# A planned attention and two-layer kernel: new durations and lags in the planner, and 32 subtractions moved from GpSimd to VectorE

## The chip, the cores and the metric

The kernel runs on one core of one Trainium2 chip. The metric is the device time of one execution in microseconds (us); where several executions were timed, their median. TensorE (PE in the rows), VectorE (DVE), ScalarE (ACT), GpSimd (POOL) and SyncE (SP) each work through a list of instructions of their own, in order, and wait for each other by semaphores. The transfers are issued by SP.

## What is computed

The reference has three parts in a row. `_attn_ref` runs a recurrence over 768 positions for 4 batches and 8 heads of 48 features: the state is multiplied by a complex number of magnitude below one, the product of key and value is added, and the query reads it. `_moe_ref` takes the 3072 rows of 384 features through `x @ w_in` (384 to 2048), a function g of the hidden values, and `g @ w_out` (back to 384). `_moe2_ref` does the same with other weights and another g:

```python
x = attn_out.transpose(0, 2, 1, 3).reshape(B * S, H * D)
h = x @ w_in;  g = np.where(h > 0.0, h, np.exp(np.minimum(h, 0.0)) - 1.0);  x = g @ w_out      # first layer
h = x @ w_in;  g = np.where(h >= 1, h, np.where(h <= -1, 0.0, (h + 1) ** 2 / 4));  y = g @ w_out  # second layer
```

The weights come as 64-bit floating-point numbers.

## The kernel before

The sequence is cut into 6 chunks of 128 positions, and each chunk into two pairs of batches: 12 units of 256 tokens. For a unit, `norm` and `prefix` make the products of the decay along the chunk on VectorE and ScalarE and write the scaled queries and keys (tiles qd, kd, QK). SP then copies these into another layout, Qs and Ks, by twelve transfers per unit (line 432). `attend` does the scores (line 444), the products with the values (454), the transposes of the keys (459) and the new state (463) on TensorE, with the mask multiplied in on VectorE (tile ssb). Its result is split into a high part xhi (a rounded type that TensorE multiplies in one pass) and the rest xlo. `layer1_tasks` takes each unit through the first layer, two hidden tiles of 128 at a time: 18 multiplications of line 201 into bank 0 or 1 (bank_72 and bank_73 in the order's rows), g on ScalarE and VectorE (lines 228 to 234), and 18 of line 211. `layer2_tasks` does the second layer for 6 groups of 512 tokens, one hidden tile at a time (lines 274 to 285).

Every weight tile is also split in two, whi and wlo. `w_tasks` loads the 64-bit words (line 175), shapes 32-bit numbers of them in three steps on VectorE (176, 178, 180), makes whi by a cast on ScalarE (182), and wlo as the difference. For the first layer the difference is made on TensorE (lines 190 and 191) and copied by ScalarE (193). For the second layer, where `lb` is None, GpSimd subtracts (line 184): 16 tiles by 2 halves, 32 instructions. The second layer's weights go into the same tiles whi and wlo as the first layer's, so each can be written only when the last unit of the first layer has used it. The words pass through st, s, r, M, qd and kd, and the 32-bit numbers through wv and ssb.

The order of all this is not written by hand. Each step is added to a `Plan` (class at line 39) with an engine, a duration in ns, a priority and what it reads and writes. `add` turns these into dependences, each with a lag: `SAME` for two steps of one engine, `CROSS` by the engine that waits, `DMA` after a transfer. `place` fills a list schedule with these numbers, forwards and backwards in turn, and `issue` emits the order of the shortest schedule it found. The numbers decide only the order; on the chip the semaphores decide when a step runs. Sixty multiplications by a tile of zeros (line 517) and twelve more (238) have no data to wait for and run where the planner puts them.

Of the kernel before, what the change touches and what calls it, by code (L numbers as in the profile page):

```python
# [16 lines left out]
B, H, S, D = 4, 8, 768, 48  # L17
C = 128
NC_ = S // C
# [14 lines left out]
def ROW(h, e):  # L34
    """Where feature (h, e) of the attention's output lies in the first layer's input."""
    return 32 * h + e if e < 32 else 256 + 32 * (h % 4) + 16 * (h // 4) + (e - 32)


class Plan:
    """A static schedule: tasks are added in an order that is right by itself, with what they read  # L40
    and write. They are placed by a list scheduler with rough durations, forwards and backwards in
    turn, and issued in the order of the shortest schedule found."""

    SAME = {"PE": 0, "DVE": 130, "ACT": 160, "POOL": 130, "SP": 0, "NONE": 0}
    CROSS = {"PE": 330, "DVE": 190, "ACT": 190, "POOL": 200, "SP": 100, "NONE": 0}     # to
    DMA = 1600
# [4 lines left out]
    def add(self, eng, ns, prio, fn, r=(), w=()):  # L51
        after, i = {}, len(self.tasks)             # task: its results are needed
# [61 lines left out]
def dve(n):  # L114
    return 70 + n / 0.96


def actv(n):
    return 95 + n / 1.2
# [3 lines left out]
def attn_moe2_kernel(ctx: ExitStack, tc: tile.TileContext, a, qk, v, w, mask, ident, nat, out):  # L123
# [40 lines left out]
    def w_tasks(add, layer, f, prio, rb, tb, lb=None):  # L164
        # float64 bits -> float32 (24 bits kept) -> a float32r part and the rest
        for p in range(2):
# [16 lines left out]
            if lb is None:  # L183
                add("POOL", 960, prio, lambda hi=hi, lo=lo, t=t: nc.gpsimd.tensor_tensor(
# [7 lines left out]
            add("PE", 800, prio, rest, r=[tk, ("whi", f, p), "ident", "nid"], w=[bkey])  # L192
# [11 lines left out]
    def y_mms(ys, fs, gt, n, lo):  # L204
        # the products with the activations' high part (lo=0) or with their low part
# [9 lines left out]
    def layer1_tasks(add, xhi, xlo, dst, dk, p0, dp, xk):  # L215
        ys = (ya[:, 0], ya[:, 1], yb)
        for p in range(NF // 2):
# [8 lines left out]
            add("PE", 1960, pr, lambda hp=hp, fs=fs: h_mms(hp, fs, xhi, xlo),  # L226
# [9 lines left out]
            if p == 0:  # L236
                # one accumulation group for the two parts of this bank
# [4 lines left out]
            add("PE", 1310, pr - 10, lambda fs=fs, g2=g2: y_mms(ys, fs, g2[0], 256, 0), r=[("ghi", mb)] + WK, w=BK[2:4])  # L242
            add("PE", 650, pr - 10, lambda fs=fs, g2=g2: y_mms(ys, fs, g2[1], 256, 1), r=[("glo", mb)] + WK, w=BK[2:4])
# [8 lines left out]
    def layer2_tasks(add, g, t2, src, sk, dst):  # L252
        # one group of 512 tokens; the first layer's activations come back from DRAM
# [13 lines left out]
        for f in range(NF):  # L267
# [6 lines left out]
            add("PE", 1960, pr + f, lambda hp=hp, f=f: h_mms(o1(hp), (f,), t2("xhi", i), t2("xlo", i)), r=XK + WK[0], w=[BK[hb]])  # L274
# [9 lines left out]
            add("PE", 1310, pr + f - 1, lambda f=f, ghi=ghi: y_mms(ys, (f,), o1(ghi()), 512, 0), r=[("ghi", mb)] + WK[1], w=YK)  # L284
            add("PE", 650, pr + f - 1, lambda f=f, glo=glo: y_mms(ys, (f,), o1(glo()), 512, 1), r=[("glo", mb)] + WK[1], w=YK)
# [7 lines left out]
    # ------------------------------------------------------------ phase 1: attention and the first layer  # L293
    with ExitStack() as c1:
# [7 lines left out]
        # these also hold the second layer's weights as they come  # L302
# [12 lines left out]
        state = T([96, 2, 2, 4, 128], "state")             # (re/im, d), pair of batches, b, pair of heads, e  # L315
# [19 lines left out]
        def norm(u, pr):  # L335
            """a -> the normalised a, in place."""
# [202 lines left out]
        def t2(name, i=0):  # L539
            return 3 if name == "n" else late[name][i]  # L540
# [172 lines left out]
```

## Time and profile before

| What | us |
|---|---|
| median of 3 executions | 1077.87 |
| lowest and highest of the three | 1070.60, 1078.63 |
| span of the profiled execution, first to last instruction | 1070.1 |
| TensorE busy | 1017.8 |
| VectorE busy | 780.3 |
| ScalarE busy | 506.9 |
| GpSimd busy | 41.2 |

The span is the stretch that the profile's rows cover; it lies 0.5 us under the lowest of the timed executions. "Busy" counts the time in which an engine had an instruction at work, and the end of a multiplication is modelled. A row of the timeline gives the start, the duration, the engine, the line, and, in square brackets, how long the engine was idle before it and what ended that wait. The duration of a short VectorE instruction includes a tail that overlaps with the next one, so what a row of such instructions costs is read from the step between their starts.

### The profile page before, as it was taken

The page shows a single profiled execution, that of the slowest core. Times are in us where ns is not written, and L with a number is a line of the kernel's source. Part 1 is how long each engine was busy: PE and PEld are TensorE (multiplying, and loading weights), DVE is VectorE, ACT ScalarE, POOL GpSimd, SP SyncE. Part 2 cuts the span into 40 slices and gives each one's busy share as a digit, 9 for nine tenths or more (in the row PEclk, how much of TensorE's full clock was granted, in tenths as well). Part 3 has the DMA queues.
Part 4 walks back from the last instruction along what each step waited for, and adds up shares of the span by engine and source line. Part 5 has one row for each costly group of instructions (what it writes and reads, how often), then busy time and mean ns, then how long its engine had stood idle before and what let it go on. Part 6 is the DMA issues. An engine that isn't in the chain of part 4 may idle for free.

```text
span 1070.1 us, 18759 instructions
## 1 busy us (share of the span) xinstructions
PE 1017.8 (95%) x7626; PEld 896.3 (84%) x7626; DVE 780.3 (73%) x1501; ACT 506.9 (47%) x942; POOL 41.2 (4%) x37
## 2 busy tenths in 40 slices
PE   4789899999999999999999989899999999999996
PEld 2469799999999999999999987688888888888885
DVE  7979898998999988988835499955454554544443
ACT  5547475565565466555534555433343333433322
POOL 0000000000000000000000044400000000000000
PEclk8699999999999999999999999999999999999999
DMA  8274624634335426346163144001010010000000
GB/s 316 70 165 136 168 57 95 124 75 105 78 98 128 79 91 119 69 99 133 23 145 102 60 151 161 17 1 59 1 59 1 1 59 1 30 0 1 31 1 33
DMA packets 44543, 84.01 MB, mean 79 GB/s; under 512 B 4512, under 2 KB 27808, under 8 KB 44448
## 3 DMA queue, kind: packets, MB, share of 16 engines
q1 hardware_dynamic: 44448, 82.72, 30.3%
q8 instruction: 62, 1.02, 0.4%
q14 instruction: 33, 0.27, 0.1%
HBM read 54.39 MB, written 9.44 MB: 60 GB/s over the span
## 4 chain that ended last, share of the span: by engine, by line
PE 73%; DVE 14%; DMA 5%; issue 3%; ACT 2%; SPq 1%; POOL 0%; DVEq 0%; ACTq 0%
PE bank L201 31%; PE bank L211 31%; PE bank L444 4%; PE bank L454 3%; PE bank L463 2%; DMA Ks<-QK 2%; DMA st<-in_w_dram 2%; DVE wv L178 1%; DVE A L322 1%; DVE wv L180 1%; DMA A<-in_a_dram 1%; PE bank L459 1%; DVE wv L176 1%; DVE mm L322 1%; DVE mo_e L231 1%
## 5 line engine op out<-in xcount | busy, mean ns | idle before, releaser
L201 PE MATMUL bank<-xhi,whi 128*128 128x256 f32 (+1 forms) x864 | 277.6, 321 | 0.7 <-DVE mo_e L231 0.7
L201 PE MATMUL bank<-xlo,whi 128*128 128x256 f32 (+1 forms) x864 | 275.8, 319 | 0.8 <-DVE xlo L322 0.8
L201 PE MATMUL bank<-xhi,wlo 128*128 128x256 f32 (+1 forms) x864 | 275.8, 319 | 0.0
L201 PEld LDWEIGHTS bank<-xhi,whi 128*128 128x128 f32 x864 | 162.9, 189 | 15.3 <-DVE mo_e L231 1.4
L201 PEld LDWEIGHTS bank<-xlo,whi 128*128 128x128 f32 x864 | 162.9, 189 | 14.3 <-DVE xlo L322 1.0
L201 PEld LDWEIGHTS bank<-xhi,wlo 128*128 128x128 f32 x864 | 162.7, 188 | 13.2
L211 PE MATMUL bank<-mo_hi,whi 128*128 128x256 f32 (+1 forms) x768 | 141.4, 313 | 6.5 <-ACT mo_hi L233 3.3
L211 PE MATMUL bank<-mo_lo,whi 128*128 128x256 f32 (+1 forms) x768 | 141.6, 313 | 2.9 <-DVE mo_lo L234 2.8
L211 PE MATMUL bank<-mo_hi,wlo 128*128 128x256 f32 (+1 forms) x768 | 138.9, 309 | 0.0
L211 PEld LDWEIGHTS bank<-mo_hi,whi 128*128 128x128 f32 x768 | 111.4, 188 | 18.6 <-ACT mo_hi L233 4.3
L211 PEld LDWEIGHTS bank<-mo_lo,whi 128*128 128x128 f32 x768 | 110.9, 189 | 14.7 <-DVE mo_lo L234 4.4
L211 PEld LDWEIGHTS bank<-mo_hi,wlo 128*128 128x128 f32 x768 | 110.9, 188 | 8.8
L228 ACT ACTIVATE mo_e<-bank 128x512 f32<-128x512 f32 x96 | 57.4, 597 | 88.8 <-PE bank L201 87.2
L277 ACT ACTIVATE mo_e<-mo_e,b_half 128x512 f32<-128x512 f32 x64 | 46.4, 724 | 87.7 <-DVE mo_e L275 87.5
L231 DVE SCALAR_TENSOR_TENSOR mo_e<-mo_e,bank 128x512 f32<-128x512 f32 x96 | 65.4, 681 | 24.6 <-ACT mo_e L230 24.0
L275 DVE TENSOR_SCALAR mo_e<-bank 128x512 f32<-128x512 f32 x64 | 44.1, 689 | 48.6 <-PE bank L201 48.6
L233 ACT CAST mo_hi<-mo_e 128x512 fp32r<-128x512 f32 x96 | 59.3, 617 | 39.5 <-DVE mo_e L231 34.7
L234 DVE TENSOR_TENSOR mo_lo<-mo_e,mo_hi 128x512 fp32r<-128x512 f32 x96 | 67.4, 702 | 14.4 <-ACT mo_hi L233 11.2
L277 ACT ACTIVATE mo<-mo,b_half 128x512 f32<-128x512 f32 x32 | 23.2, 724 | 88.0 <-DVE mo L275 88.0
L281 DVE TENSOR_TENSOR mo_lo<-mo_e,mo_hi 128x512 fp32r<-128x512 f32 x64 | 44.1, 690 | 27.5 <-ACT mo_hi L280 26.2
L275 DVE TENSOR_SCALAR mo<-bank 128x512 f32<-128x512 f32 x32 | 22.1, 690 | 57.8 <-PE bank L201 57.8
L230 ACT ACTIVATE mo_e<-mo_e 128x512 f32<-128x512 f32 x96 | 60.8, 633 | 1.6
(122 smaller groups left out, 1519.7 us busy)
## 6 DMA issues: line engine op xcount, KB each, us to landing
st<-in_w_dram SPq DMA_DIRECT2D x28, 384.0 KB, 3.8
A<-in_a_dram SPq DMA_DIRECT2D x12, 768.0 KB, 6.0
QK<-in_qk_dram SPq DMA_DIRECT2D x12, 768.0 KB, 4.5
V<-in_v_dram SPq DMA_DIRECT2D x12, 448.0 KB, 5.3
M<-in_w_dram SPq DMA_DIRECT2D x12, 384.0 KB, 4.1
Qs<-qd SPq DMA_DIRECT2D x36, 128.0 KB, 3.9
Ks<-kd SPq DMA_DIRECT2D x36, 128.0 KB, 4.2
Ks<-QK SPq DMA_DIRECT2D x36, 128.0 KB, 4.9
```

The costliest lines, as they stand in the source:

```text
L201: pe.matmul(out=hp[:, j], lhsT=wt[:, ks], rhs=xt[:, k], start=(i == 0), stop=(i == 8))
L211: pe.matmul(out=ys[mt], lhsT=wt[f][:, ms], rhs=gt[:, j], start=(f == 0 and not lo and wt is whi and whole), stop=(f == NF - 1 and lo == 1 ...
L228: add("ACT", actv(512), pr - 200, lambda hb=hb, e=e: act.activation(out=e, in_=hps[hb], func=AF.Relu, scale=-1.0), r=[BK[hb]], w=[("e", mb)])
L230: add("ACT", actv(512), pr - 200, lambda e=e: act.activation(out=e, in_=e, func=AF.Exp, scale=-1.0), w=[("e", mb)])
L231: add("DVE", dve(512), pr - 200, lambda hb=hb, e=e: vec.scalar_tensor_tensor(out=e, in0=e, scalar=-1.0, in1=hps[hb], op0=ALU.add, op1=ALU. ...
L233: add("ACT", actv(512), pr - 200, lambda e=e, ghi=ghi: act.copy(out=ghi, in_=e), r=[("e", mb)], w=[("ghi", mb)])
L234: add("DVE", dve(512), pr - 200, lambda e=e, ghi=ghi, glo=glo: vec.tensor_tensor(out=glo, in0=e, in1=ghi.bitcast(F32), op=ALU.subtract), r ...
L275: add("DVE", dve(512), pr + f - 2, lambda hp=hp, e=e: vec.tensor_scalar(out=e(), in0=hp, scalar1=-1.0, scalar2=1.0, op0=ALU.max, op1=ALU.m ...
L277: add("ACT", actv(512), pr + f - 2, lambda e=e: act.activation(out=e(), in_=e(), func=AF.Square, scale=0.5, bias=b_half), w=[("e", mb)])
L281: add("DVE", dve(512), pr + f - 2, lambda e=e, ghi=ghi, glo=glo: vec.tensor_tensor(out=glo(), in0=e(), in1=ghi().bitcast(F32), op=ALU.subt ...
L444: pe.matmul(out=s_ps[:, j * 128:(j + 1) * 128], lhsT=Ks[:, h, b], rhs=Qs[:, h, b], start=True, stop=True)
L454: pe.matmul(out=o[32 * j:32 * j + 32], lhsT=lhsT, rhs=rhs, start=(not old and not (part and hg)), stop=(old == (c > 0) and not (part and n ...
```

## The change

The planner gets other numbers. The durations of the TensorE steps and of ScalarE are set anew, the lags depend on the engine that waits (`CROSS`) and, where TensorE is the producer, on it too (`FROM`). The lag after a transfer depends on the tile it writes: 4200 ns for Qs and Ks, 3900 for A and V, 2900 for all others, where it was 1600 for every one. The 32 subtractions of the second layer's wlo go from GpSimd to VectorE and are planned with `dve(384)`. No step is added or dropped. Comments are gone, and lines from the class on lie 8 lower at most: line 184 is 192 after the change, 432 is 440, 201 is 209.

```diff
-    SAME = {"PE": 0, "DVE": 130, "ACT": 160, "POOL": 130, "SP": 0, "NONE": 0}
-    CROSS = {"PE": 330, "DVE": 190, "ACT": 190, "POOL": 200, "SP": 100, "NONE": 0}     # to
-    DMA = 1600
+    SAME = {"PE": 0, "DVE": 118, "ACT": 135, "POOL": 130, "SP": 0, "NONE": 0}
+    CROSS = {"PE": 110, "DVE": 128, "ACT": 120, "POOL": 180, "SP": 50, "NONE": 0}
+    FROM = {"PE": 90}
+    DMA = {"Qs": 4200, "Ks": 4200, "A": 3900, "V": 3900}
...
-            lags.append((t, self.DMA if e == "SP" else self.CROSS[eng] if e != eng else self.SAME[e] if data else 0))
-        self.tasks.append((eng, ns, prio, fn, lags))
+            if e == "SP":
+                lag = self.DMA.get(self.tasks[t][5], 2900)
+            elif e != eng:
+                lag = self.CROSS[eng] + self.FROM.get(e, 0)
+            else:
+                lag = self.SAME[e] if data else 0
+            lags.append((t, lag))
+        name = w[0] if w else None
+        self.tasks.append((eng, ns, prio, fn, lags, name[0] if isinstance(name, tuple) else name))
...
-    return 95 + n / 1.2
+    return 70 + n / 1.2
...
-                add("POOL", 960, prio, lambda hi=hi, lo=lo, t=t: nc.gpsimd.tensor_tensor(
+                add("DVE", dve(384), prio, lambda hi=hi, lo=lo, t=t: vec.tensor_tensor(
                     out=lo, in0=t.bitcast(F32), in1=hi.bitcast(F32), op=ALU.subtract), r=[tk, ("whi", f, p)], w=[("wlo", f, p)])
...
-            add("PE", 1960, pr, lambda hp=hp, fs=fs: h_mms(hp, fs, xhi, xlo),
+            add("PE", 2115, pr, lambda hp=hp, fs=fs: h_mms(hp, fs, xhi, xlo),
```

The other TensorE durations change in the same way: 1310 to 1408 and 650 to 706 or 702 for line 211, 800 to 970 for lines 190 and 191, 880 to 910 for the scores, 1190 and 900 to 1010 and 560 for the values, 340 to 300 and 1250 to 1320 for lines 459 and 463.

What this does to the order is shown at three places. The first is SP's list near the program's start, where the queries and keys of the first unit are copied into Qs and Ks (st are weight words on their way in). Before:

```order
L175 DMA st_127<-in_w_dram 128x768
L432 DMA Qs<-qd_144 16x8x256
L175 DMA st_128<-in_w_dram 128x768
L432 DMA Qs<-qd_144 16x8x256 x2
L175 DMA st_127<-in_w_dram 128x768
L432 DMA Ks<-kd_145 16x8x256 x3
L432 DMA Ks<-QK 16x8x256 x3
L432 DMA Qs<-QK 16x8x256 x3
L338 DMA A_151<-in_a_dram 128x1536
```

SP's list at the same place after the change:

```order
L183 DMA st_128<-in_w_dram 128x768
L440 DMA Qs<-qd_144 16x8x256 x3
L440 DMA Qs<-QK 16x8x256 x3
L440 DMA Ks<-kd_145 16x8x256 x3
L440 DMA Ks<-QK 16x8x256 x3
L346 DMA A_151<-in_a_dram 128x1536
```

The second half of Qs moved ahead of both halves of Ks, and the last three transfers are now those of Ks.

The second place is TensorE's list where it first uses them: transposes of keys into bank_79, scores into bank_76, and the zero multiplications into bank_74. Before:

```order
L517 MATMUL bank_74<-zero 128x512 x9
L459 MATMUL bank_79<-id_sb,Ks 128x96 x4
L517 MATMUL bank_74<-zero 128x512 x3
L238 MATMUL bank_74<-zero 128x512
L459 MATMUL bank_79<-id_sb,Ks 128x96 x4
L444 MATMUL bank_76<-Qs,Ks 128x128 x4
L463 MATMUL bank_79<-V_153,kt 96x48 x8
```

TensorE's list there after the change:

```order
L246 MATMUL bank_74<-zero 128x512
L198 MATMUL bank_79<-wv_126,id_sb 128x384
L199 MATMUL bank_79<-whi_100,nid 128x384
L467 MATMUL bank_79<-id_sb,Ks 128x96 x4
L452 MATMUL bank_76<-Qs,Ks 128x128 x4
L467 MATMUL bank_79<-id_sb,Ks 128x96 x4
L452 MATMUL bank_76<-Qs,Ks 128x128 x4
```

The first scores now follow the first four transposes; the zero multiplications and the second four transposes that stood between them moved.

The third place is VectorE's list soon after the last unit's xlo, where the second layer's weights are made beside the last unit's g (mo_e, mo_lo). Before:

```order
L231 SCALAR_TENSOR_TENSOR mo_e_129<-mo_e_129,bank_72 128x512
L176 TENSOR_SCALAR ssb_147<-s_142 128x384
L178 SCALAR_TENSOR_TENSOR ssb_147<-s_142,ssb_147 128x384
L234 TENSOR_TENSOR mo_lo_133<-mo_e_129,mo_hi_131 128x512
L180 SCALAR_TENSOR_TENSOR ssb_147<-s_142,ssb_147 128x384
L231 SCALAR_TENSOR_TENSOR mo_e_130<-mo_e_130,bank_73 128x512
L176 TENSOR_SCALAR ssb_147<-M 128x384
L178 SCALAR_TENSOR_TENSOR ssb_147<-M,ssb_147 128x384
L180 SCALAR_TENSOR_TENSOR ssb_147<-M,ssb_147 128x384
L234 TENSOR_TENSOR mo_lo_134<-mo_e_130,mo_hi_132 128x512
```

VectorE's list there after the change:

```order
L239 SCALAR_TENSOR_TENSOR mo_e_129<-mo_e_129,bank_72 128x512
L186 SCALAR_TENSOR_TENSOR ssb_147<-s_142,ssb_147 128x384
L188 SCALAR_TENSOR_TENSOR ssb_147<-s_142,ssb_147 128x384
L242 TENSOR_TENSOR mo_lo_133<-mo_e_129,mo_hi_131 128x512
L192 TENSOR_TENSOR wlo_112<-ssb_147,whi_96 128x384
L184 TENSOR_SCALAR ssb_147<-M 128x384
L239 SCALAR_TENSOR_TENSOR mo_e_130<-mo_e_130,bank_73 128x512
L186 SCALAR_TENSOR_TENSOR ssb_147<-M,ssb_147 128x384
L192 TENSOR_TENSOR wlo_109<-wv_126,whi_93 128x384
L184 TENSOR_SCALAR wv_126<-s_141 128x384
L242 TENSOR_TENSOR mo_lo_134<-mo_e_130,mo_hi_132 128x512
```

The subtractions (L192) stand between the other steps, each a step or more behind the L188 that finishes its input; GpSimd's list has none left.

## Rows read from the trace of the kernel before

**Rows 1.** The page: span, and TensorE's busy time.

```profile
span 1070.1 us, 18759 instructions
PE 1017.8 (95%) x7626; PEld 896.3 (84%) x7626; DVE 780.3 (73%) x1501; ACT 506.9 (47%) x942; POOL 41.2 (4%) x37
```

**Rows 2.** Six stretches: length, busy us of PE, PEld, DVE, ACT, POOL, clock, DMA.

```profile
0.00:64.63 64.63, 41.16 (x106) 24.54 (x106) 57.02 (x140) 30.82 (x61) 2.01 (x5) 0.79 0.61 181
64.63:80.10 15.47, 14.26 (x153) 12.19 (x153) 10.77 (x31) 9.12 (x21) 0.00 (x0) 0.89 0.59 192
80.10:137.30 57.20, 53.32 (x412) 46.64 (x413) 52.87 (x117) 35.83 (x76) 0.00 (x0) 0.97 0.54 143
137.30:612.85 475.55, 470.15 (x4976) 457.37 (x4975) 399.29 (x816) 260.52 (x510) 1.03 (x1) 1.00 0.42 93
612.85:695.30 82.45, 72.60 (x421) 61.50 (x420) 78.60 (x128) 40.26 (x73) 38.14 (x31) 1.00 0.35 115
695.30:1070.10 374.80, 366.26 (x1565) 294.08 (x1563) 181.73 (x273) 130.32 (x203) 0.00 (x0) 0.99 0.06 20
```

**Rows 3.** SP's timeline, the issues of the first unit's last copies.

```profile
56.94 1.83 SPq L432 DMA_DIRECT2D Ks<-QK  x3
58.87 3.07 SPq L432 DMA_DIRECT2D Qs<-QK  x3
```

**Rows 4.** TensorE's timeline, first use of Ks and Qs.

```profile
64.63 0.68 PE L459 MATMUL bank<-id_sb,Ks 96*128 96x96 f32 x4 [3.60 <-DMA Ks<-QK]
...
66.86 0.85 PE L459 MATMUL bank<-id_sb,Ks 96*128 96x96 f32 x4
67.50 1.46 PE L444 MATMUL bank<-Qs,Ks 96*128 96x128 f32 x8
```

**Rows 5.** VectorE's timeline: first mask multiplication, second xlo of units 0 and 1.

```profile
68.99 0.69 DVE L322 TENSOR_TENSOR ssb<-bank,mask_sb 128x512 f32<-128x512 f32 x1 [5.23 <-PE bank L444]
79.49 0.55 DVE L322 TENSOR_TENSOR xlo<-bank,xhi 128x384 fp32r<-128x384 f32 x1
136.88 0.55 DVE L322 TENSOR_TENSOR xlo<-bank,xhi 128x384 fp32r<-128x384 f32 x1
```

**Rows 6.** What TensorE waited for, 60 to 612 us: total, times, longest.

```profile
PE bank L459 <- DMA Ks<-QK: 3.6, 1, 3.6
PE bank L444 <- DMA Ks<-QK: 2.2, 2, 1.2
PE bank L444 <- DMA st<-in_w_dram: 1.9, 1, 1.9
...
PE bank L444 <- DMA V<-in_v_dram: 0.5, 1, 0.5
```

**Rows 7.** What VectorE waited for, 80.1 to 137.3 us.

```profile
DVE wv L176 <- DMA st<-in_w_dram: 2.6, 3, 1.0
```

**Rows 8.** VectorE's timeline between the layers: long and short instructions of equal form.

```profile
616.20 1.25 DVE L180 SCALAR_TENSOR_TENSOR ssb<-M,ssb 128x384 uint32<-128x384 uint32 x1
...
620.48 0.35 DVE L176 TENSOR_SCALAR wv<-st 128x384 uint32<-128x384 uint32 x1
...
621.82 0.55 DVE L178 SCALAR_TENSOR_TENSOR wv<-st,wv 128x384 uint32<-128x384 uint32 x1
622.28 1.16 DVE L176 TENSOR_SCALAR ssb<-r 128x384 uint32<-128x384 uint32 x1
...
689.63 0.77 DVE L180 SCALAR_TENSOR_TENSOR ssb<-r,ssb 128x384 uint32<-128x384 uint32 x1
```

**Rows 9.** GpSimd's timeline, one of the 32 subtractions.

```profile
621.98 1.25 POOL L184 TENSOR_TENSOR wlo<-wv,whi 128x384 fp32r<-128x384 f32 x1 [2.23 <-ACT whi L182]
```

**Rows 10.** What TensorE waited for, 612 to 700 us.

```profile
PE bank L211 <- ACT mo_hi L233: 3.3, 4, 1.4
PE bank L211 <- ACT mo_hi L280: 3.2, 1, 3.2
```

**Rows 11.** GpSimd's waits over the whole span; the longest is the first.

```profile
POOL wlo L184 <- ACT whi L182: 650.6, 27, 607.3
```

More of the change, by code (lines that the diff above doesn't have):

```diff
@@ L191, in rest @@
                 pe.matmul(out=bk[:, 0:DM], lhsT=nid, rhs=hi, start=False, stop=True)
-            add("PE", 800, prio, rest, r=[tk, ("whi", f, p), "ident", "nid"], w=[bkey])
+            add("PE", 970, prio, rest, r=[tk, ("whi", f, p), "ident", "nid"], w=[bkey])
             add("ACT", actv(384), prio, lambda lo=lo, bk=bk: act.copy(out=lo, in_=bk[:, 0:DM]), r=[bkey], w=[("wlo", f, p)])
@@ L241, in layer1_tasks @@
             WK = [(n, f, 1) for n in ("whi", "wlo") for f in fs]
[L242 to L243 removed]
+            add("PE", 1408, pr - 10, lambda fs=fs, g2=g2: y_mms(ys, fs, g2[0], 256, 0), r=[("ghi", mb)] + WK, w=BK[2:4])
+            add("PE", 706, pr - 10, lambda fs=fs, g2=g2: y_mms(ys, fs, g2[1], 256, 1), r=[("glo", mb)] + WK, w=BK[2:4])
         i = count["st"] % 2
@@ L273, in layer2_tasks @@
             WK = [[(n, f, p) for n in ("whi", "wlo")] for p in range(2)]
-            add("PE", 1960, pr + f, lambda hp=hp, f=f: h_mms(o1(hp), (f,), t2("xhi", i), t2("xlo", i)), r=XK + WK[0], w=[BK[hb]])
+            add("PE", 2110, pr + f, lambda hp=hp, f=f: h_mms(o1(hp), (f,), t2("xhi", i), t2("xlo", i)), r=XK + WK[0], w=[BK[hb]])
             add("DVE", dve(512), pr + f - 2, lambda hp=hp, e=e: vec.tensor_scalar(
@@ L283, in layer2_tasks @@
             YK = [BK[y] for y in yi]
-            add("PE", 1310, pr + f - 1, lambda f=f, ghi=ghi: y_mms(ys, (f,), o1(ghi()), 512, 0), r=[("ghi", mb)] + WK[1], w=YK)
-            add("PE", 650, pr + f - 1, lambda f=f, glo=glo: y_mms(ys, (f,), o1(glo()), 512, 1), r=[("glo", mb)] + WK[1], w=YK)
+            add("PE", 1408, pr + f - 1, lambda f=f, ghi=ghi: y_mms(ys, (f,), o1(ghi()), 512, 0), r=[("ghi", mb)] + WK[1], w=YK)
+            add("PE", 702, pr + f - 1, lambda f=f, glo=glo: y_mms(ys, (f,), o1(glo()), 512, 1), r=[("glo", mb)] + WK[1], w=YK)
         for m in range(3):
@@ L470, in attend @@
                     sb = ssb[sb_i]
-                    add("PE", 880, pr - 50, lambda b=b, hg=hg: scores(b, hg), r=QSB + KSB, w=[BK[4]])
+                    add("PE", 910, pr - 50, lambda b=b, hg=hg: scores(b, hg), r=QSB + KSB, w=[BK[4]])
                     tt(pr - 150, 512, sb, s_ps.rearrange("p (j t) -> p j t", j=4),
                        mask_sb.rearrange("p (o t) -> p o t", o=1).to_broadcast([128, 4, 128]), ALU.mult, [BK[4]], [("ssb", sb_i)])
-                    add("PE", 1190 if c > 0 else 900, pr - 50, lambda b=b, hg=hg, sb=sb: values(b, hg, sb),
+                    add("PE", 1010 if c > 0 else 560, pr - 50, lambda b=b, hg=hg, sb=sb: values(b, hg, sb),
                         r=[("ssb", sb_i), vb] + (QSB + [("state", bp, b)] if c > 0 else []), w=[BK[5 + b]])
```

4 lines of the change are left out of this document (2 added, 2 removed).

## The prediction

> **What bounds the kernel now.** The page comes first: TensorE is busy for 1017.8 of 1070.1 us [rows 1], so all that a new order can win lies in 52.3 us, and the next question is where they lie. I cut the span at the first use of Ks, at the first two finished units, at the end of the first layer's even part and where the second layer begins [rows 2]. Up to 64.63 us TensorE mostly waits for work or multiplies zeros, and VectorE, busy for 57.02, sets the pace together with the copies into Ks and Qs. From 64.63 to 80.10 the first unit goes through the attention in a chain. In the two stretches from 80.10 to 612.85 TensorE loses 57.20 - 53.32 = 3.88 and 475.55 - 470.15 = 5.40. Between the layers, 612.85 to 695.30, it loses 82.45 - 72.60 = 9.85, and there VectorE is the fullest engine: 78.60 of 82.45. From 695.30 on TensorE is busy but for 8.54, most of which is the last transfers and the last checks; VectorE has half its time to spare, and neither the lags after a transfer nor the subtractions matter there. The granted clock is 0.97 to 1.00 of full speed (2.4 GHz) from 80.10 on, so I carry nothing for the clock behind that point; before it, it is 0.79 and 0.89. What ends TensorE's waits I read next [rows 4, 6, 10], then VectorE's timeline around them [rows 5, 7, 8].
>
> **Start.** TensorE's first transposes of Ks begin at 64.63 after 3.60 of waiting for Ks; the first scores follow only at 67.50 [rows 4]. Three zero multiplications, one of line 238 and four more transposes stand between them, and the last Qs are issued after the last Ks, from 58.87 with 3.07 us for the three [rows 3]. In the new order Qs goes ahead of Ks, and the scores come right behind four transposes. The four before them cost the step from 66.86 to 67.50, 0.64. If Ks lands as before, the scores begin at 64.63 + 0.64 = 65.27, 2.2 earlier, and the mask multiplication that waited 5.23 for them [rows 5] with them. From there to the second xlo VectorE has about the same work in both orders, 0.4 less in the new one by the steps of its instructions. Together -2.6. When Ks lands is not known: its three issues took 1.83 and the three of Qs 3.07 [rows 3], so with Qs in front Ks could come some 3 us later (term +0.4), or, if the cheaper place behind Qs costs it nothing and k' is ready sooner, some 2.4 earlier (-5). I take -2.6, since VectorE finishes k' at about the same place in its list.
>
> **First layer.** TensorE's waits that a transfer ends are, behind the first scores, 2.2 + 1.9 + 0.5 = 4.6 [rows 6]. The planner allowed 1600 ns from the end of an issue to the data; the gap from the last Ks issue (56.94 + 1.83 = 58.77) to the transposes at 64.63 is 5.9, so 4200 is nearer to the chip, and it now keeps other work for such times. But from 80.10 to 137.30 VectorE is nearly as full (52.87) as TensorE (53.32), and the next unit's first layer begins with its second xlo, at 136.88 [rows 5]. The new order puts 128 instructions where 117 stood before that one: 11 x 52.87 / 117 = 5.0 us more. It gives TensorE 28 multiplications more ahead of the same place: 28 x 53.32 / 412 = 3.6. So this stretch gains nothing, though three VectorE waits of 2.6 for st [rows 7] shrink. I take -3.5 from the later units alone: 1.9 + 0.5 of transfer waits, some 0.3 of the waits for Ks, and 0.8 of the steps that wait for VectorE because its lag was too long or short in the plan. If the plan's better lags fill every gap that is not VectorE's, it is -9.3 (3.88 + 5.40), and if the 5.0 us fall on the path whole while TensorE's 3.6 cover only part, and nothing else comes, +3: a range of -9.3 to +3.
>
> **Between the layers.** 32 subtractions leave GpSimd; one takes 1.25 there [rows 9]. On VectorE the same shapes step by 0.46 to 0.55 (from 621.82 to 622.28 it is 0.46) [rows 8], so 32 x 0.47 = 15.0 us go onto an engine with 82.45 - 78.60 = 3.85 to spare. Against this stands what GpSimd costs VectorE now: 27 of its instructions last about 0.81 longer than their like, each while a GpSimd subtraction runs, as the step of line 176 at 622.28 (1.16 against 0.35 at 620.48) and those of line 180 at 616.20 (1.25) and, shorter, at 689.63 (0.77) [rows 8]. Summed over the 27 this is 18.1 us. Only instructions that read no bank are hit, those that read one never. The net is 15.0 - 18.1 = -3.1 on VectorE, which is the engine that sets this stretch. In the trace TensorE waits there 3.3 for mo_hi of line 233 and 3.2 for the second layer's first mo_hi [rows 10]; both follow VectorE through mo_e and the weights. With the engine 3.1 lighter, and planned with a duration that is right (960 stood for GpSimd's 1.25), I take both waits as nearly gone: -6.5. All of the 9.85 could go (lower end); if the wait moves to the cast on ScalarE that each subtraction now sits behind, only -2 is left, which I take as the likely upper end; the case beyond it is the second rival. GpSimd waited 650.6 for these casts in all, 607.3 of it before the first [rows 11].
>
> The Trainium skill speaks against this edit on the page "Perfetto Trace Analysis", section "Optimizing Scalar/DVE Operations": where DVE is saturated, work may better go off it, even to GpSimd, though the two share a read port, so that moving work between them might not help. By its first half the edit is +15.0 on the fullest engine; by its second half what GpSimd does is not free for DVE. The lengthened rows show the second half at work here, and 18.1 against 15.0 decides narrowly for the move. [...]
>
> **Second layer.** Its order on TensorE is that of before but for where it begins, and no wait there hangs on a lag that moved: 0, within 1 either way.
>
> **The sum.** -2.6 - 3.5 - 6.5 + 0 = -12.6. The profiled execution spans 1070.1, and so would come to 1057.5. That span lies 0.5 under the lowest of the three runs and 7.8 (0.7%) under their median of 1077.87; the difference applied to the median gives 1065.3, and I forecast 1065.
>
> **Rivals.** First, VectorE bounds the first layer too. For it: 52.87 against 53.32 in the second unit's stretch, and the 11 instructions more. Against it: from 137.30 on it is busy for 399.29 of 475.55 only. Then the start's gain and the stage's are eaten there, and the 6.5 are cut to about 5: 1073.
>
> Second, slower: VectorE works in order, so a subtraction whose cast is late stops what is queued behind it, the steps of mo_e and mo_lo that TensorE waits for. In the new list it often stands only one or two instructions behind the step that finishes its input, while ScalarE needs the cast (and its own queue) in between. GpSimd's waits but the longest come to (650.6 - 607.3) / 26 = 1.67 each, and nobody stood behind it. VectorE can take 3.85 of idle and the 3.1 gained; with the 6.1 of the other terms 13.05 in all, or 0.41 a subtraction. Beyond 0.41 the kernel gets slower. At 0.8, half of what GpSimd had, it is 32 x 0.8 - 13.05 = +12.6: 1090. Against it: the planner knows the cast, with a lag of 120 to 128, and mostly puts another instruction of some 0.5 between.
>
> Third, the numbers change the order and not the time: TensorE's list is bound by the same last wait at each place, and what one transfer no longer costs another does; the four terms then cancel to within 3: 1078, for which the few and short waits of TensorE speak.
>
> **Chances.** The forecast's case 0.68, the first rival 0.18, the second 0.06, the third 0.08. A measurement of this kernel can tell about 1% (10.8 us) from no change. The forecast's case reaches from 1053 (all four terms at their lower ends: -5 - 9.3 - 9.85 - 1 = -25.2) to 1072, and 0.10 of its 0.68 lies above 1067; the first and third rival lie within 1%, but for 0.01 above; the second is slower. So faster 0.58, within 1% 0.35, slower 0.07. The range from 1053 to 1077 leaves out the second rival, half of the third and the forecast's lowest tail.
>
> **What would show it.** Right: the first scores near 65.3 and the second xlo near 76.9; TensorE's waits for Ks, st and V gone but for the first; no VectorE instruction of the lines of 176 to 180 above 0.8 us; GpSimd idle from the start on; TensorE's loss between the layers under 4; the second layer as long as before. Wrong: VectorE's waits for whi at the moved subtraction adding up to more than 6 (second rival); the stretch from the first to the second unit longer than 57.20 by several us (first rival); the first scores later than 67.5, because Ks now lands last; waits for mo_hi of line 233 as long as before.

## The result and the profile after the change

The changed kernel takes 1062.95 us (median of four executions, 1059.36 to 1065.68); the kernel before, with one more execution beside it, 1075.32 (1070.60 to 1078.63). The ratio is 0.9895, with a 95% interval of 0.9856 to 0.9934: faster by 1.05%, or some 12 us. A second job with six executions gave 0.9889 (0.9866 to 0.9912). The forecast was 1065 with a range of 1053 to 1077, that is -12.6 us, and the time lies in it. The sum came out right; of its three terms one was right in kind, and the other two were not. The profiled execution shows how.

The page of the changed kernel, to be read beside [rows 1]:

```profile
span 1063.9 us, 18684 instructions
PE 1020.5 (96%) x7626; PEld 901.5 (85%) x7626; DVE 779.4 (73%) x1533; ACT 507.6 (48%) x942; POOL 2.0 (0%) x5
```

The same six stretches as in [rows 2], cut at the same events (the first use of Ks, the first layer's start in two units, the end of its even part, the second layer's start), though not at the same number of multiplications, as the counts show: length, then busy us of PE, PEld, DVE, ACT, POOL, the granted clock, and the DMA engines' share and rate. The seventh row is a piece of the fourth, right behind a wait.

```profile
0.00:63.66 63.66, 41.38 (x110) 24.61 (x110) 56.54 (x141) 30.03 (x60) 2.01 (x5) 0.79 0.65 185
63.66:80.85 17.19, 16.81 (x145) 14.77 (x146) 10.95 (x35) 8.81 (x21) 0.00 (x0) 0.60 0.43 155
80.85:142.16 61.31, 57.91 (x457) 50.19 (x456) 59.88 (x129) 40.23 (x82) 0.00 (x0) 1.00 0.51 137
142.16:614.59 472.43, 463.11 (x4883) 450.47 (x4882) 392.68 (x793) 254.39 (x496) 0.00 (x0) 0.99 0.44 94
614.59:690.00 75.41, 75.41 (x477) 67.71 (x476) 72.23 (x151) 42.95 (x77) 0.00 (x0) 1.00 0.40 126
690.00:1063.90 373.90, 365.85 (x1564) 293.76 (x1562) 187.11 (x288) 131.17 (x208) 0.00 (x0) 0.99 0.06 20
...
362.08:366.00 3.92, 3.92 (x20) 3.92 (x21) 1.85 (x4) 1.77 (x4) 0.00 (x0) 0.56 0.58 216
```

Read the difference of the first two numbers of a row, which is TensorE's idle time, against [rows 2]: 22.28 for 23.47 at the start, 0.38 for 1.21 in the first unit, 3.40 for 3.88 in the second, 9.32 for 5.40 in the other units, nothing for 9.85 between the layers, 8.05 for 8.54 at the end. Together idle time fell by 8.9 us. But TensorE was busy for 2.7 us more (1020.5 against 1017.8) with the same 7626 multiplications: the clock of the second row is 0.60, where [rows 2] had 0.89, and its busy time is 2.6 us longer. So the span fell by 6.2 only. This profiled execution is the slowest of the four (1065.68), and that of before the fastest (1070.60), so the profile shows half of what the medians show.

Between the layers VectorE now runs like this (its timeline, with the moved subtraction in the second row):

```profile
629.64 0.55 DVE L186 SCALAR_TENSOR_TENSOR wv<-st,wv 128x384 uint32<-128x384 uint32 x1
630.11 0.55 DVE L192 TENSOR_TENSOR wlo<-wv,whi 128x384 fp32r<-128x384 f32 x1
630.58 0.55 DVE L188 SCALAR_TENSOR_TENSOR wv<-st,wv 128x384 uint32<-128x384 uint32 x1
```

The subtraction steps by 0.47 us, as estimated, and no instruction is lengthened as those of [rows 8] were. What VectorE waits for between 605 and 700 us, in all, times, longest:

```profile
DVE wlo L192 <- ACT whi L190: 2.2, 2, 1.2
```

Two of the 32 subtractions wait for their cast, 2.2 us together: the second rival's mechanism is there, at a sixth of the 13 us from which it would have decided.

And in the other units, TensorE's waits from 142 to 615 us, which answer to [rows 6]:

```profile
PE bank L452 <- DMA Ks<-QK: 6.2, 3, 2.3
PE bank L452 <- DVE ssb L330: 1.0, 1, 1.0
PE bank L219 <- ACT mo_hi L241: 0.9, 2, 0.6
```

The waits for st and V are gone. The planner now allows 4200 ns for Ks, and yet the waits for Ks grew from 2.2 to 6.2 us.

### The profile page after: what moved, and what is told of

The parts are those of the page before. It is cut to its first block, busy times and chain, and to the rows that moved or that the text cites. A ratio compares the mean times of both kernels' runs of the same rounds, so it can differ in the third digit from the quotient of the medians.

```text
span 1063.9 us, 18684 instructions
## 1 busy us (share of the span) xinstructions
PE 1020.5 (96%) x7626; PEld 901.5 (85%) x7626; DVE 779.4 (73%) x1533; ACT 507.6 (48%) x942; POOL 2.0 (0%) x5
## 3 DMA queue, kind: packets, MB, share of 16 engines
q8 instruction: 62, 1.02, 0.4%
## 5 line engine op out<-in xcount | busy, mean ns | idle before, releaser
L219 PEld LDWEIGHTS bank<-mo_hi,whi 128*128 128x128 f32 x768 | 111.8, 189 | 11.7 <-ACT mo_hi L241 1.3
L241 ACT CAST mo_hi<-mo_e 128x512 fp32r<-128x512 f32 x96 | 59.4, 618 | 43.7 <-DVE mo_e L239 42.3
L242 DVE TENSOR_TENSOR mo_lo<-mo_e,mo_hi 128x512 fp32r<-128x512 f32 x96 | 65.7, 685 | 11.8 <-ACT mo_hi L241 11.5
L452 PE MATMUL bank<-Qs,Ks 96*128 96x128 f32 x384 | 56.1, 292 | 8.2 <-DMA Ks<-QK 6.2
L288 ACT CAST mo_hi<-mo_e 128x512 fp32r<-128x512 f32 x64 | 39.8, 622 | 46.0 <-DVE mo_e L287 45.8
L452 PEld LDWEIGHTS bank<-Qs,Ks 96*128 96x128 f32 x384 | 50.2, 203 | 11.7 <-issue 6.4
```

Of the source, the lines that this page charges most:

```text
L219: pe.matmul(out=ys[mt], lhsT=wt[f][:, ms], rhs=gt[:, j], start=(f == 0 and not lo and wt is whi and whole), stop=(f == NF - 1 and lo == 1 ...
L241: add("ACT", actv(512), pr - 200, lambda e=e, ghi=ghi: act.copy(out=ghi, in_=e), r=[("e", mb)], w=[("ghi", mb)])
L242: add("DVE", dve(512), pr - 200, lambda e=e, ghi=ghi, glo=glo: vec.tensor_tensor(out=glo, in0=e, in1=ghi.bitcast(F32), op=ALU.subtract), r ...
L288: add("ACT", actv(512), pr + f - 2, lambda e=e, ghi=ghi: act.copy(out=ghi(), in_=e()), r=[("e", mb)], w=[("ghi", mb)])
L452: pe.matmul(out=s_ps[:, j * 128:(j + 1) * 128], lhsT=Ks[:, h, b], rhs=Qs[:, h, b], start=True, stop=True)
```

## Experiments: which half of the change made the gain

**The move alone, and the numbers alone.** The two parts of the diff were run apart. The first kernel is the one before with the new lines for the subtraction only:

```diff
-                add("POOL", 960, prio, lambda hi=hi, lo=lo, t=t: nc.gpsimd.tensor_tensor(
+                add("DVE", dve(384), prio, lambda hi=hi, lo=lo, t=t: vec.tensor_tensor(
```

> Numbers of the kernel before, but the 32 subtractions planned and issued on VectorE. Theory 1, the gain between the layers comes from the move (VectorE freed of the 18.1 us of lengthened instructions, subtraction planned with a true duration): TensorE's waits from the last unit to the second layer's start, 9.9 us before, fall under 4, the time falls by 5 to 10 us, 1065 to 1070. Theory 2, it comes from the new numbers: the waits stay near 10 and the time is that of before within 4 us, 1071 to 1079.

Measured: 1060.59 us, ratio 0.9893 (0.9864 to 0.9922). Its first unit, and its stretch from the last unit into the second layer:

```profile
64.70:83.00 18.30, 18.17 (x152) 16.05 (x152) 9.94 (x28) 8.62 (x20) 0.00 (x0) 0.65 0.46 153
608.50:688.00 79.50, 79.50 (x493) 71.07 (x492) 71.40 (x146) 42.07 (x76) 0.00 (x0) 1.00 0.39 120
```

In the second row TensorE is busy for 79.50 of 79.50: all idle time between the layers is gone, by the move alone, and the time is that of the full change, 11.7 us under the kernel before in the same job, where at most 10 were expected.

Idle time understates this. In the traces of these two kernels TensorE's multiplications have the same order up to number 5535, and again for the last 1442; between these lie the same 649 in two orders. Their stretch in the kernel before, then in the move alone (the rows count two more that reach into it):

```profile
600.04:723.91 123.87, 114.02 (x651) 97.29 (x650) 99.79 (x162) 56.84 (x103) 39.16 (x32) 1.00 0.24 78
602.10:712.50 110.40, 110.40 (x651) 97.15 (x650) 97.47 (x196) 57.61 (x104) 0.00 (x0) 1.00 0.28 86
```

The move made them 13.5 us shorter: 9.85 of that was idle time, and 3.6 stood in TensorE's busy time, though the work and the clock are the same.

The second kernel is the changed one with that edit taken back, so it has the new numbers and GpSimd:

> New numbers, the subtractions left on GpSimd and planned there with 960. Theory 1 (the move makes the gain): about 9 us of TensorE waits between the layers, some 20 VectorE instructions there lengthened by about 0.8 us, and a time of 1070 to 1077, since the rest of the order gave nothing in the changed kernel. Theory 2 (the numbers make it): waits there under 3 us, 1060 to 1066.

Measured: 1085.06 us, ratio 1.0116 (1.0078 to 1.0154). The numbers by themselves make the kernel slower, beyond what either theory expected. TensorE's multiplications have the same order as in the changed kernel, so the stretch between the layers can be cut at the same ones; the changed kernel's stands second. Then follow four instructions of VectorE and two of GpSimd in it:

```profile
613.70:710.07 96.37, 81.71 (x477) 70.23 (x476) 83.96 (x135) 44.68 (x82) 37.63 (x32) 0.96 0.31 99
614.59:690.09 75.50, 75.50 (x478) 67.75 (x476) 72.32 (x151) 43.04 (x77) 0.00 (x0) 1.00 0.40 126
```

```profile
640.53 1.16 DVE L184 TENSOR_SCALAR wv<-s 128x384 uint32<-128x384 uint32 x1
...
643.51 0.35 DVE L184 TENSOR_SCALAR wv<-st 128x384 uint32<-128x384 uint32 x1
...
650.33 0.35 DVE L184 TENSOR_SCALAR wv<-M 128x384 uint32<-128x384 uint32 x1
650.60 0.35 DVE L184 TENSOR_SCALAR wv<-kd 128x384 uint32<-128x384 uint32 x1
```

```profile
640.16 1.31 POOL L192 TENSOR_TENSOR wlo<-wv,whi 128x384 fp32r<-128x384 f32 x1 [1.51 <-ACT whi L190]
641.44 1.13 POOL L192 TENSOR_TENSOR wlo<-ssb,whi 128x384 fp32r<-128x384 f32 x1
```

TensorE is idle for 96.37 - 81.71 = 14.7 us there, 4.8 more than in the kernel before, and the stretch takes 96.37 - 75.50 = 20.9 us longer than in the changed kernel. The two profiled spans, 1084.3 and 1063.9, differ by 20.4: all that this kernel is behind lies between the layers. The instruction at 640.53 lasts 1.16 us while GpSimd subtracts from 640.16 to 641.47; the one at 643.51, of the same form and with GpSimd idle until 643.61, lasts 0.35, as do the last two, which step by 0.27. In this trace 27 VectorE instructions are lengthened, by 18.8 us in all.

**The same order, with either engine.** TensorE's order is shared by those two kernels; VectorE's and ScalarE's differ between the layers, because the planner places a subtraction of 960 ns on GpSimd in another way. To hold everything else still, the changed kernel's plan was kept, and only the call put on GpSimd:

```diff
-                add("DVE", dve(384), prio, lambda hi=hi, lo=lo, t=t: vec.tensor_tensor(
+                add("DVE", dve(384), prio, lambda hi=hi, lo=lo, t=t: nc.gpsimd.tensor_tensor(
```

> The order of the changed kernel word for word, only that GpSimd runs the subtractions at the places planned for VectorE. Theory 1: VectorE loses 32 x 0.47 = 15 us of work and gets back about 18 us of lengthened instructions, of the lines that shape the weights' words above all; net some +3 us on an engine with 3.2 us to spare in 75.4, and GpSimd's 1.25 comes later than 0.47: 2 to 8 us of TensorE waits return, 1065 to 1071. Theory 2 (the order alone matters): no waits, 1061 to 1065.

Measured: 1071.05 us, ratio 0.9971 (0.9946 to 0.9995). The same stretch, cut at the same multiplications:

```profile
614.34:694.81 80.47, 78.05 (x477) 67.86 (x476) 70.67 (x123) 42.23 (x77) 32.22 (x27) 1.00 0.37 118
```

TensorE is idle for 2.4 us where the changed kernel was never idle, and the stretch takes 5.0 us longer (80.47 for 75.50). Twenty instructions are lengthened, by 12.4 us, of which VectorE, 15 us of subtractions lighter, can carry most. The profiled spans, 1069.3 and 1063.9, differ by 5.4, and both first units ran at half clock; so nearly all of the difference is GpSimd's, between the layers. By the medians this kernel is 8 us behind the changed one; where the other 3 us lie was not traced. Of the 20.9 us that the kernel with the numbers alone loses, then, 5.0 come with GpSimd in a given order, and 15.9 with the other order of VectorE and ScalarE that the planner made for it.

The other way round, the order of the kernel before with the call on VectorE, at the places planned for GpSimd:

```diff
-                add("POOL", 960, prio, lambda hi=hi, lo=lo, t=t: nc.gpsimd.tensor_tensor(
+                add("POOL", 960, prio, lambda hi=hi, lo=lo, t=t: vec.tensor_tensor(
```

> The order of the kernel before word for word, planned for GpSimd with 960, only that VectorE runs the 32 subtractions at the places in the program where GpSimd's were issued. If the gain is VectorE's relief from 18 us of lengthened instructions, TensorE's waits between the layers fall to under 5 and the time to 1062 to 1068 although nothing was planned for it. If the plan of the subtraction makes the gain, VectorE waits for ScalarE's casts in front of the subtractions (over 5 us in all) and the time stays at 1070 to 1078.

Measured: 1069.33 us, ratio 0.9939 (0.9915 to 0.9962). The first unit and the stretch between the layers:

```profile
64.70:87.30 22.60, 22.60 (x152) 19.68 (x153) 11.06 (x31) 9.55 (x21) 0.00 (x0) 0.50 0.40 128
612.60:692.20 79.60, 75.92 (x462) 66.76 (x461) 75.45 (x161) 41.97 (x77) 0.00 (x0) 0.98 0.37 120
```

TensorE's idle time between the layers falls from 9.85 to 79.60 - 75.92 = 3.7 with nothing planned for it, and no instruction is lengthened. The time is between the two cases expected. The 649 multiplications from above, which stand here in the order of the kernel before, give the share:

```profile
606.20:725.02 118.82, 114.23 (x651) 98.50 (x650) 96.53 (x194) 57.02 (x103) 0.00 (x0) 0.99 0.25 82
```

They take 118.82 us, 5.1 less than before, where the move alone took 13.5 less; a fall of the clock from 678.6 to 682.0 us is in it, which costs 1.7, so that it would be 6.8 without it. By the ratios it is 0.61% of 1.07%. So about half of the gain is VectorE's relief, and the rest comes with planning the subtraction as VectorE's.

**A truer duration for GpSimd.** Could the planner have been told instead? The kernel with the numbers alone, with 1250 in place of 960:

> New numbers, subtractions on GpSimd, planned with 1250 ns instead of 960, near what they last there. If the 1085 us of the new numbers alone come from the short duration, TensorE's waits between the layers fall from 15 to under 8 and the time to 1070 to 1077. If they come from GpSimd lengthening VectorE's instructions, which no duration of GpSimd tells the planner, about 26 instructions are still lengthened by 0.7 us each, the waits stay at 10 or more and the time at 1078 or more.

Measured: 1084.39 us, ratio 1.0076 (1.0050 to 1.0102).

```profile
615.50:702.30 86.80, 71.73 (x438) 62.55 (x437) 79.33 (x129) 41.92 (x78) 40.57 (x32) 0.94 0.34 109
```

The loss is 15.1 us, 26 instructions are lengthened by 17.5 us, VectorE is busy for 79.33 of 86.80. The second of the expected cases holds: neither 960 nor 1250 ns on GpSimd tells the planner what the subtraction costs, since the cost falls on VectorE's instructions.

## Experiments: the first unit and the clock

In the changed kernel TensorE begins the first unit a microsecond earlier than before, and the scores come 3.5 us earlier than the 67.50 of [rows 4]. Its timeline:

```profile
63.66 0.52 PE L467 MATMUL bank<-id_sb,Ks 96*128 96x96 f32 x4 [1.65 <-issue]
64.02 1.08 PE L452 MATMUL bank<-Qs,Ks 96*128 96x128 f32 x8
64.94 0.56 PE L467 MATMUL bank<-id_sb,Ks 96*128 96x96 f32 x4
65.88 2.08 PE L452 MATMUL bank<-Qs,Ks 96*128 96x128 f32 x8 [0.38 <-DVE ssb L330]
```

The first scores take 1.08 us, the second, of the same form, 2.08: the clock has fallen to half (1.2 GHz), and it stays there until about 79, although TensorE has hardly a gap (16.81 busy of 17.19). This is VectorE's row of the second xlo of the first unit, which [rows 5] has at 79.49:

```profile
80.03 0.56 DVE L330 TENSOR_TENSOR xlo<-bank,xhi 128x384 fp32r<-128x384 f32 x1 [0.30 <-ACT xhi L337]
```

That is 0.5 us later, where the forecast had it 2.6 earlier. In the kernel before, zero multiplications stood behind the first transposes [rows 4], and the clock came back after them, from 0.50 between 66 and 68 us to 1.00 from 70 on. They do not decide it: the move alone and the run with VectorE in GpSimd's place have the order of the kernel before on TensorE here, the same zeros with it, and ran this unit at 0.65 and 0.50 (their rows above). To test whether TensorE's own work decides, eight more of them were put into the wait (the order is otherwise that of the changed kernel):

```diff
             def turn(b, hg):
+                for _ in range(0 if first else 8):
+                    pe.matmul(out=banks[3], lhsT=zero, rhs=zero[:, 0:1].to_broadcast([128, 512]), start=True, stop=True)
+                first.append(1)
```

> The changed kernel with 8 more multiplications of zeros right ahead of the first transposes of Ks, where TensorE stood idle from 62.0 to 63.66 us. If the clock of 1.2 GHz from 65 to 79 us in the changed kernel comes from what TensorE did before, the granted clock of 64 to 79 us rises from 0.6 to 0.85 or more, scores take 1.1 instead of 2.05 us, the first layer starts at 76 to 78 instead of 80.65, and the time falls by 2 to 4 us. Rival: VectorE sets the second unit anyway; then the clock rises but the second unit's first layer still begins near 142 and the time stays within 1 us. Second rival: the clock is not in TensorE's hand here, and nothing changes.

Measured: 1060.08 us, ratio 0.9893 (0.9870 to 0.9916), so no gain that can be told from the changed kernel's. In its profiled execution the first unit ran at full clock, in 11.28 us:

```profile
63.48:74.76 11.28, 10.78 (x144) 9.38 (x145) 10.11 (x33) 8.50 (x21) 0.00 (x0) 1.00 0.66 237
```

But the mean clock of its four executions was 0.986, 0.976, 0.979 and 0.982, and the time followed it (1058.87, 1063.21, 1060.37, 1059.79): one good profile is no proof. The changed kernel itself, run again, settles what the good profile is worth:

> The changed kernel once more, beside the other two on one chip. With the first unit's clock left to chance its executions spread over 4 us or more, 1059 to 1066, at a ratio of 0.987 to 0.992 to the kernel before; the two with zeros spread less. If the spread does not come from there, all three spread alike.

Measured: 1061.57 us (1055.91 to 1065.40), ratio 0.9889. The profiled execution is the fastest of the six. TensorE's timeline of the same four rows, and the first unit:

```profile
63.90 0.52 PE L467 MATMUL bank<-id_sb,Ks 96*128 96x96 f32 x4 [1.19 <-ACT wlo L201]
64.26 1.08 PE L452 MATMUL bank<-Qs,Ks 96*128 96x128 f32 x8
65.18 0.49 PE L467 MATMUL bank<-id_sb,Ks 96*128 96x96 f32 x4
66.12 1.16 PE L452 MATMUL bank<-Qs,Ks 96*128 96x128 f32 x8 [0.45 <-DVE ssb L330]
```

```profile
63.90:75.20 11.30, 10.83 (x145) 9.43 (x145) 9.95 (x32) 8.49 (x21) 0.00 (x0) 1.00 0.66 237
```

The same instructions in the same order, behind a wait of 1.19 us instead of 1.65, and the clock holds: the unit takes 11.30 us where the other execution of the same kernel needed 16.99 (63.66 to its first multiplication of the first layer at 80.65), 5.7 us more. The whole spans are 1054.1 and 1063.9. So this kernel's executions differ by chance in the clock of the first unit: 5.7 of the 9.8 us between these two lie there. The other execution also had a second fall of the clock, from 464.6 to 468.0 us. The next two stretches of the faster one, that is the second unit and the other units:

```profile
75.16:135.70 60.54, 57.81 (x459) 50.54 (x458) 60.35 (x131) 40.05 (x82) 0.00 (x0) 1.00 0.50 139
135.70:604.73 469.03, 461.02 (x4883) 448.77 (x4882) 392.34 (x793) 254.60 (x496) 0.00 (x0) 1.00 0.44 94
```

The kernel before meets the same chance: the 15.47 us of [rows 2] are from the fastest of its executions, while TensorE in the same order took 18.30 and 22.60 us in the two rows named above (19.4 and 22.8 when cut at the same multiplication), and 23 executions of it in one job went from 1070.85 to 1079.53 us.

More zero multiplications, sixteen in a wait of 4.1 us, were then put into the kernel of the move alone:

> Numbers of the kernel before, subtractions on VectorE, and 16 multiplications of zeros ahead of the first transposes of Ks, where TensorE stood idle for 4.1 us. If the clock after that idle time is what made the first unit long (83.0 instead of 79.0 us in the run of the move alone, whose order there is that of before), the granted clock of the first unit is 0.9 or more, its first layer starts at 75 to 78, and the time is 1053 to 1058, under the changed kernel's 1063. Rival: the zeros only fill the wait and the clock falls as before in most runs: 1059 to 1063, as the move alone.

Measured: 1057.20 us, ratio 0.9830 (0.9801 to 0.9858), and its six executions lie within 1.4 us (1056.15 to 1057.57), where the move alone had 5.5 (1058.33 to 1063.82). Its first unit:

```profile
64.60:78.30 13.70, 12.57 (x152) 10.90 (x152) 9.73 (x28) 8.51 (x20) 0.00 (x0) 1.00 0.60 204
```

In these six executions nothing is left of the spread; they are too few to say that the clock cannot fall there.

## Experiments: the waits for Ks

The seventh row of the changed kernel's stretches shows what a wait for Ks costs beside itself. TensorE waited for 2.32 us until 362.08; in the 3.92 us behind it the clock was 0.56, which is 3.92 x 0.44 = 1.7 us more. (Behind the two other long waits for Ks, of 1.97 us at 410.37 and 1.95 at 510.61, the clock stayed whole.) The planned 4200 ns count from the end of an issue, for which the planner has 650, so in the plan a copy lands 4.85 us after its issue begins. The copies from QK take longer as a rule; the medians from issue to landing are the last column of the changed kernel's DMA issues:

```profile
Qs<-QK SPq DMA_DIRECT2D x36, 128.0 KB, 5.1
Ks<-kd SPq DMA_DIRECT2D x36, 128.0 KB, 4.6
Ks<-QK SPq DMA_DIRECT2D x36, 128.0 KB, 5.3
```

So the lag of both was raised in the changed kernel:

```diff
-    DMA = {"Qs": 4200, "Ks": 4200, "A": 3900, "V": 3900}
+    DMA = {"Qs": 6500, "Ks": 6500, "A": 3900, "V": 3900}
```

> The changed kernel with 6500 instead of 4200 ns planned for the copies into Qs and Ks (measured medians from issue to landing 3.8 to 5.3 us, and TensorE waited 6.2 us for Ks in three units). If these waits come from a lag that is still too short, they fall under 2 us, the falls of the clock behind them go too, and the time falls by 5 to 9 us, 1054 to 1058. Rival: the planner's order is of one piece and another number moves the loss elsewhere: other TensorE waits of 4 us or more in the first layer, 1060 to 1066.

Measured: 1063.06 us, ratio 0.9875 (0.9834 to 0.9916). TensorE's waits:

```profile
PE bank L467 <- ACT kt L488: 3.4, 2, 2.2
PE bank L462 <- DVE ssb L330: 3.0, 1, 3.0
PE bank L452 <- DVE ssb L330: 2.0, 3, 0.8
```

No wait for Ks is left, and waits for kt and ssb took their place, as the rival had it; the first unit of its profiled execution ran at 0.65. With ten zero multiplications as above added to it:

> The changed kernel with 6500 ns for Qs and Ks (TensorE's waits in the first layer 12.3 instead of 17.4 us, but a first unit at half clock) and 10 multiplications of zeros ahead of the first transposes. If the clock of the start took what the lag gave, the first unit runs at 0.9 or more, its first layer starts near 76 instead of 87.8, and the time is 1052 to 1057. Rival: the dip that the long lag cost comes from elsewhere and the time stays at 1059 or more.

Measured: 1056.94 us (1055.53 to 1062.17), ratio 0.9846 (0.9822 to 0.9870). The first unit was at 0.81, better than 0.65 and short of the expected 0.9, and one of five executions fell back to 1062. Last, the kernel of the move and sixteen zeros was given the lags of the change, and nothing else of its numbers:

```diff
-    DMA = 1600
+    DMA = {"Qs": 4200, "Ks": 4200, "A": 3900, "V": 3900}
...
-            lags.append((t, self.DMA if e == "SP" else self.CROSS[eng] if e != eng else self.SAME[e] if data else 0))
+            lags.append((t, self.DMA.get(self.tasks[t][5], 2900) if e == "SP" else self.CROSS[eng] if e != eng else self.SAME[e] if data else 0))
```

> The numbers of the kernel before with only the transfer lags of the change (4200, 3900, 2900), the subtractions on VectorE and 16 multiplications of zeros: tells what the lags are worth in a plan that is otherwise that of the fastest run, 1057.2. If lags near the measured landing help by themselves, TensorE's waits that a transfer ends (4.0 in that run) fall under 2 and the time to 1053 to 1056. Rival, as in the changed kernel: the planner trades them for other waits or a low clock, 1056 to 1064.

Measured: 1055.22 us (1054.99 to 1056.37), ratio 0.9819 (0.9802 to 0.9836): the lowest median of all, and faster than the changed kernel (0.9889 in the same job). Against the same kernel without the lags (1057.20, ratio 0.9830, in another job) it is 2 us lower, but the intervals of the two ratios overlap, so that a gain from the lags is not shown. Its stretches from the first unit to the second layer:

```profile
67.60:81.60 14.00, 12.84 (x151) 10.53 (x150) 12.66 (x33) 9.72 (x24) 0.00 (x0) 1.00 0.44 152
81.60:138.40 56.80, 51.77 (x409) 44.55 (x407) 53.74 (x120) 36.22 (x73) 0.00 (x0) 1.00 0.56 140
138.40:604.90 466.50, 463.56 (x4927) 451.06 (x4926) 393.31 (x798) 256.90 (x501) 0.00 (x0) 1.00 0.43 95
604.90:684.30 79.40, 79.40 (x492) 71.00 (x491) 71.97 (x147) 42.80 (x77) 0.00 (x0) 1.00 0.37 120
```

TensorE loses 2.9 us in the third row, where the changed kernel lost 9.3 and the kernel before 5.4, and the clock is full throughout. Its waits behind the start that a transfer ends are 2.3 us, where they were 4.0 without the lags, which is near to the 2 us expected; the wait for mo_lo fell too, from 3.5 to 2.5. Since the planner made another order of the whole from these numbers, the difference can't be put down to one wait.

## Why the prediction was right, point by point

**Start, forecast -2.6: wrong in the profiled execution, by chance of the clock.** The scores did come earlier, at 64.02 instead of 67.50, more than the 65.27 that was worked out. The step that failed is the one from the scores to the second xlo, which were to come earlier together: it took for granted that the instructions between keep their durations. At half clock the second xlo was at 80.03; in the execution that kept its clock it was at 74.91, 4.6 earlier than before. The prediction set the clock aside only from 80.10 us on and showed 0.89 ahead of that, but priced nothing for it; its 0.64 for four transposes is itself a step at half clock, and took 0.36 at full clock (63.66 to 64.02). What a chance of this kind is worth is the 5.7 us between two executions of one kernel.

**First layer, forecast -3.5: wrong in sign.** TensorE's idle time behind the first unit went from 3.88 + 5.40 = 9.28 to 3.40 + 9.32 = 12.72, +3.4, a little outside the range's upper end of +3, and one of the three long waits for Ks is followed by a fall of the clock besides; in the execution whose clock held it went to 2.73 + 8.01 = 10.74, +1.5. The step that failed is the reading that a planned lag nearer to the 5.9 us between the issue's end and the data's use makes the waits smaller. The waits for st and V went, as forecast, but those for Ks grew by 4.0. A lag of 4200 is still short of 5.9, and the lags between engines were shortened with it, so that the planner may have packed the rest closer up to the transfers; this is a reading that no run shows by itself, though with the transfer lags alone the waits for transfers were 2.3 for 4.0. What was said of the second unit held: VectorE got more instructions (129 for 117) and sets the stretch (59.88 of 61.31), which became longer (57.20 to 61.31), and TensorE did more work in it (457 multiplications for 412), so that its loss there stayed about the same, 3.40 for 3.88.

**Between the layers, forecast -6.5: right in kind, too small.** All of the 9.85 went, the forecast's lower end, and on the same 649 multiplications the move alone gave 13.5, which is beyond it: idle time was taken for all that can be won, and TensorE's busy time for fixed. The lengthening of VectorE's instructions is shown by three pairs: none with the subtractions on VectorE, 20 to 27 with them on GpSimd, in two planner's orders and with the order held. One lasts 18.1 / 27 = 0.67 us longer on the mean; the 0.81 of the prediction is that of the longer ones, and its sum of 18.1 holds. The step that was too cautious is the net: -3.1 us on VectorE was taken to buy about 6.5 of TensorE's waits, while the move alone bought all. About half of this is relief, and the rest the plan.

The rule of the Trainium skill that was weighed against the edit, on the page "Perfetto Trace Analysis", section "Optimizing Scalar/DVE Operations", that moving work between these two engines might not help, is not borne out here in this direction: with the order held, 1071.05 on GpSimd and 1062.95 on VectorE. On the page "SBUF — State Buffer", section "Who interferes with whom", the Trainium skill names `tensor_scalar` among the operations that can use both port pairs in a faster mode, and so can contend with GpSimd. Line 176, a `tensor_scalar` with one input, is lengthened [rows 8], and undisturbed it steps by 0.27 us for 384 elements (650.33 to 650.60 in the run of the numbers alone), where the two-input steps of that size take 0.47, so these rows and the page agree.

**The sum.** -2.6, -3.5 and -6.5 were forecast. In the profiled execution the start cost instead of giving, the first layer cost about 3.4 in idle time, and the stretch between the layers gave 9.85 in idle time. By the runs of the two halves the forecast had the cause half right: it counted on 6.1 us from the numbers, and the numbers gave nothing on top of the move (0.9893 alone, 0.9895 together). The forecast's -12.6 came out because one term was too small by about what the two others were too large, and that is luck. So is the clock's part in it: against the 1070.1 of the kernel before, the two profiled executions of the changed kernel give -6.2 and -16.0, and -12.4 between the medians lies between them. Of the rivals the first showed its sign, a second unit longer by 4.1 us (3.3 in the execution whose clock held), but not its 1073. The second, waits behind the cast, is measured at 2.2 us. The third, that the numbers bring nothing, is true of the numbers and not of the move.

Open remains one part of why the new numbers without the move are as slow as 1085. The 20.4 us between the profiled spans lie between the layers, where the clock also fell (0.83 from 680 to 700 us). With the order of the changed kernel GpSimd cost 5.0 of them; which places in the other order of VectorE and ScalarE make the rest wasn't tried.

## What to carry to other kernels

A small share of busy time on GpSimd can be dear: look in VectorE's timeline for pairs of one form with two durations, sum the excess, and compare it with what the moved work would cost there (18 us against 15 here). Where the engine that is relieved sets the pace, the gain can be larger than that balance: 3 us on VectorE went with 13.5 us on the chain. To tell what a stretch gained, compare the time of the same instructions, not idle time alone. A planner's number that is nearer to the trace is not by itself an order that is nearer to the best; run the numbers and the move apart, and where a wait stands ahead of TensorE's chain of small multiplications, look at the clock behind it in several executions before a gain of a few microseconds is put down to the order.

## What the runs showed of the hardware

In the changed kernel the clock fell to half behind waits of TensorE of 1.65 and 2.32 us, and at 464.6 us behind two of 1.02 and 0.61, and did not fall behind 1.19, 1.95 and 1.97. In the run with GpSimd in the changed kernel's order it fell behind waits of 1.42 and 0.45 us at 62.4 and 65.6 us; in the kernel before it stayed whole behind the 3.2 us of [rows 10]. So in these traces the length of a wait alone does not tell whether the clock falls. In the changed kernel's first unit it stayed at half for 14 us in which TensorE worked with hardly a gap (idle 0.38 of 17.19 us), on transposes and multiplications with 96 rows or columns. The Trainium skill, on the page "TensorE: Matmul & The Clock Gate", Part 1, calls the slow multiplications at a kernel's start variable from run to run; here one kernel met the clock differently in its middle too, 11.30 us against 16.99 for one unit. Sixteen multiplications by zeros in the wait went with a spread of the executions of 1.4 us (six of them) where it had been 5.5 (four).

While GpSimd subtracted, instructions of VectorE that read no bank were lengthened (1.16 us for 0.35, say). In these traces no instruction that reads a bank was lengthened, and none while GpSimd was idle.
